# Decoding of the first MoE weight: lower parts on GpSimd, 14 pieces per 18 tiles, one tile between load and first step

## The chip, the cores and the metric

The kernel runs on one core of one Trainium2 chip. The metric is the device time of one execution in microseconds; the figure for the kernel before is the median of three runs. Engines are named as in the profile: PE (TensorE, with PEld for its weight loads), DVE (VectorE), ACT (ScalarE), POOL (GpSimd), SP (SyncE, which here only issues DMAs).

## The reference

An attention with a thresholded softmax, and behind it a two-layer MoE block with a Mish gate:

```python
scores = scale * q @ k.T                      # 8 batches, 8 heads, 576 x 576, head 64
thresh = max(scores) - tau
scores = where(scores >= thresh, scores, -1e9)
attn   = softmax(scores)                      # exp, row sum, division
x      = (attn @ v)  as (4608, 512)
h      = x @ w_in                             # w_in: 512 x 2048
out    = (h * tanh(softplus(h))) @ w_out      # w_out: 2048 x 512
```

q, k and v are given in float32. The two weights are given in float64 and reach the chip as 64-bit words; the chip turns them into float32 itself ("decoding", below).

## The kernel before

**Attention in tiles.** The 64 heads are taken as 32 pairs; a pair gives 9 tiles of 128 x 576 scores, so there are 288 tiles, numbered g. One loop over g (`for g in range(NT + 5)`) issues for each g a bit of work of several tiles in a fixed program order that every compute engine keeps (the wrapper at line 93 chains the instructions of each engine). Per tile: score matmuls on PE into `s`; the row maximum on DVE (`st<-s`); three small DVE operations; the exponential on ACT (`e<-s,st`); the masking with the row sum on DVE (`p<-s,st,e`); the normalisation on POOL (`p<-p,st`, in the next tile); transposes on PE two tiles later (`tp<-ident,p`) and their copies out on ACT (`pf<-tp`; from the fifth pair on `hi<-tp`, with a subtraction `lo<-tp,hi` on DVE); then the product with v on PE. The maximum of tile g+1 stands behind the masking of tile g on DVE.

**The first GEMM.** When the four pairs of a batch are through, `x @ w_in` for it runs as a stream of matmuls that the loop draws from: for tile g of the first batch `MIX_FIRST[(g - 36) % 36]` matmuls, from g = 42 on (6, 14, 22, 6, 16, 4, 12, 4, 15, 9, 16, 13, 7, 12, 5, 10 for tiles 42 to 57). Each product is made from a rounded upper part and a lower part of both factors: three matmuls, `xh*w1h`, `xl*w1h`, `xh*w1l`. So all of `w1h` and `w1l` must be there by the time the stream asks for them. Later the second GEMM, line 848, fills PE to the end.

**The decoding of w_in.** It goes by 32 pieces of 128 x 256 values. A piece needs a buffer `dec` (the pool has five, used in turn: piece i + 5 takes the buffer of piece i), and these steps, each in a tile of its own:

- its load, one DMA on SP's queue, `dec<-w_in` (line 127);
- *first*: two ACT operations (`dec<-dec`);
- *clamp*: one DVE operation; in the next tile *shift* and *sign*, two DVE operations, and *add*, one POOL operation (all `dec<-dec`);
- after one free tile, *upper*: an ACT copy `w1h<-dec`, and *lower*: the subtraction `w1l<-dec,w1h`, on POOL in the same tile or, for the nine pieces named in `ONV`, on DVE one tile later.

A table says in which tiles of each 18 a piece is begun; `LAG` puts empty tiles between the load and *first*:

```python
if weights and g % 18 in W1_STEPS:
    decoding.append([()] * LAG + weights.pop(0)())
...
if d + j * ND in ONV:
    middle = [skip] * 3
    middle[ONP] = lambda: work.lower(nc.vector)
    last = [(work.upper,), middle]
else:
    last = [(lambda: (work.upper(), work.lower(nc.gpsimd)),)]
return [(work.first, skip), *spread(work, STAGES[(d + j) % 2]), *THIRD, *last]
```

With LAG = 2, a piece begun (loaded) in tile s has *first* in s+3, *clamp* in s+4, *shift* and *sign* in s+5, *upper* and *lower* in s+7 (lower in s+8 on DVE). The 32 pieces are begun in tiles 1, 3, 4, 6, 7, 8, 10, 12, 13, 15, 16, 17, and so on by 18, the last in tile 48. The DMA waits for the *lower* of the piece that had the buffer before it.

**Order inside a tile.** ACT: exponential; *first*; copies of y (`x<-y`) and the splits of the next pairs' q, k and v (`q<-r`, `k<-r`); *upper*; the copies out of the transposes. POOL: normalisation; the subtractions of these splits (`q<-r,q`, `k<-r,k`, `vs<-r,vs`, `xl<-x,xh`); *lower*; *add*. DVE: the small operations of the maximum; the reciprocal; *clamp*; *shift*, and before tile 39 (`JOIN`) *sign*; the masking; the maximum of the next tile.

Of the kernel before, what the change touches and what calls it, by code (L numbers as in the profile page):

```python
# [15 lines left out]
B, H, S, D = 8, 8, 576, 64  # L16
NP = H // 2
LOADS = ((1, 0, 1, 3, 2, 3, 7, 3, 5, 8), (0, 3, 3, 2, 5, 4, 5, 8, 5, 7), (0, 0, 2, 4, 5, 4, 7, 6, 7, 8))
W1_STEPS = (1, 3, 4, 6, 7, 8, 10, 12, 13, 15, 16, 17)
STAGES = ((0, 1, 1), (0, 1, 1))  # L20
THIRD = ((),)
LAG = 2
XSPLIT = (4, 1, 2)
ORDER = (0, 0)
PIECES = (3, 3, 3, 3, 4, 2, 3, 4, 3)
# [1 line left out]
FULL = NP  # L27
UNV = 54
ONP = 1
ONV = (3, 9, 11, 12, 14, 15, 17, 18, 22)  # L30
JOIN = 39
PLAIN = (1,)
DM, DF = 512, 2048
# [125 lines left out]
def attention_moe(tc, q, k, v, tau, w_in, w_out, out):  # L159
# [3 lines left out]
    with ExitStack() as outer:  # L163
# [12 lines left out]
        with ExitStack() as first:  # L176
# [6 lines left out]
            with ExitStack() as att:  # L183
# [17 lines left out]
                def decode_w1(d, j):  # L201
# [5 lines left out]
                    work.load(w_in[d * P:(d + 1) * P, sl])  # L207
                    if d + j * ND in ONV:
                        middle = [skip] * 3
# [343 lines left out]
                for g in range(NT + 5):  # L553
# [70 lines left out]
                    for work in loads.pop(g, []):  # L624
                        chores.setdefault(max(g + 2, 2), []).append(work())
                    if weights and g % 18 in W1_STEPS:
                        decoding.append([()] * LAG + weights.pop(0)())
                    if g < NT:
# [270 lines left out]
```

## Time and profile before

| | |
|---|---|
| median of 3 runs | 1373.96 us (1373.25 to 1374.07) |
| profiled execution | 1371.94 us, of which the span of the program's instructions is 1370.2 us |
| granted TensorE clock | 0.996 |
| PE, PEld busy | 99%, 89% |
| DVE, ACT, POOL busy | 73%, 69%, 56% |
| decoding of w_in | from 6.8 us (first load) to about 192 us (last lower part) |

Times inside the execution count from the start of the span. A busy share of the whole span is a mean over stages with different limits, so the stages are read apart in the prediction. A row such as `e<-s,st x288` is a group: the names are the program's (what is written, what is read), then the count. A row of the timeline has start, duration, engine, operation, and in brackets the idle time of the engine before it and what ended that.

### The profile page before, as it was taken

What the parts mean: (1) busy time and instruction counts of PE and PEld (TensorE: products, weight loads), DVE (VectorE), ACT (ScalarE), POOL (GpSimd) and SP (SyncE); (2) the same over time, 40 slices, a digit from 0 to 9 for tenths busy, and PEclk for the clock granted to TensorE, in tenths of its full rate; (3) what the DMA queues carried; (4) which work ended last, traced back from release to release, by engine and by line L of the source; (5) the groups of instructions that cost most, each with busy time, mean ns of one, the idle gap of its engine ahead of it and who ended that gap; (6) DMA issues with size and microseconds to landing.
All of it is one profiled execution on the core that took longest, in us unless ns stands there. A gap on an engine that the chain in (4) does not pass through costs nothing. (4 is left out here: it accounts for less than half of the span.)

```text
span 1370.2 us, 27693 instructions
## 1 busy us (share of the span) xinstructions
PE 1352.5 (99%) x8839; PEld 1225.8 (89%) x8839; DVE 1000.6 (73%) x2976; ACT 944.0 (69%) x2106; POOL 774.0 (56%) x1115
## 2 busy tenths in 40 slices
PE   9998999999999999999999999999999999999999
PEld 7555899999999999999999999999987888888888
DVE  5999999999999999999999999957874332232210
ACT  5788788888888888888888888856555543443210
POOL 4778888778788787887887878732460000000000
PEclk9999999999999999999999999999999999999999
DMA  4333423333333233332332423128655553543310
GB/s 142 100 96 109 121 79 116 108 96 103 101 99 115 89 121 93 111 105 99 103 111 88 121 93 107 64 86 279 194 164 154 150 151 103 143 132 99 95 52 23
DMA packets 126017, 154.64 MB, mean 113 GB/s; under 512 B 23472, under 2 KB 109488, under 8 KB 125872
## 3 DMA queue, kind: packets, MB, share of 16 engines
q1 hardware_dynamic: 124720, 148.16, 36.2%
q10 hardware_dynamic: 1152, 4.72, 0.9%
q8 instruction: 70, 1.15, 0.3%
q14 instruction: 75, 0.61, 0.1%
HBM read 105.64 MB, written 47.19 MB: 112 GB/s over the span
## 5 line engine op out<-in xcount | busy, mean ns | idle before, releaser
L848 PE MATMUL o<-g,w2h 128*128 128x512 f32 (+1 forms) x1280 | 363.7, 370 | 0.6 <-DVE g L681 0.6
L93 PE MATMUL h<-xh,w1h 128*128 128x288 f32 x1024 | 302.3, 295 | 1.0 <-ACT hst L93 0.6
L93 PE MATMUL h<-xl,w1h 128*128 128x288 f32 x1024 | 302.2, 295 | 0.0
L93 PE MATMUL h<-xh,w1l 128*128 128x288 f32 x1024 | 302.2, 295 | 0.0
L93 POOL TENSOR_SCALAR p<-p,st 128x576 f32<-128x576 f32 x288 | 244.9, 850 | 58.6 <-DVE st L93 37.2
L848 PEld LDWEIGHTS o<-g,w2h 128*128 128x128 f32 x1280 | 231.6, 188 | 43.4 <-DVE g L681 1.1
L93 PE MATMUL s<-k,q 128*128 128x288 f32 (+1 forms) x1280 | 255.0, 324 | 7.9 <-DVE p L93 5.8
L93 DVE SCALAR_TENSOR_TENSOR p<-s,st,e 128x576 f32<-128x576 f32 x288 | 235.0, 816 | 20.6 <-ACT e L93 11.0
L93 ACT ACTIVATE e<-s,st 128x576 f32<-128x576 f32 x288 | 214.4, 744 | 35.5 <-DVE st L93 30.2
L848 PE MATMUL o<-g,w2l 128*128 128x512 f32 (+1 forms) x640 | 236.1, 369 | 0.0
L93 DVE TENSOR_REDUCE st<-s 128x1 f32<-128x576 f32 x288 | 216.6, 752 | 6.7 <-PE s L93 6.6
L93 PEld LDWEIGHTS s<-k,q 128*128 128x128 f32 (+1 forms) x1280 | 182.5, 189 | 37.4 <-DVE p L93 21.8
L93 DVE TENSOR_TENSOR lo<-tp,hi 128x512 fp32r<-128x512 f32 (+1 forms) x280 | 174.7, 632 | 48.0 <-ACT hi L93 41.0
L93 PEld LDWEIGHTS h<-xh,w1h 128*128 128x128 f32 x1024 | 192.6, 188 | 1.9 <-ACT hst L93 1.0
L93 PEld LDWEIGHTS h<-xh,w1l 128*128 128x128 f32 x1024 | 192.5, 188 | 0.0
L93 PEld LDWEIGHTS h<-xl,w1h 128*128 128x128 f32 x1024 | 192.5, 188 | 0.0
L93 PE MATMUL tp<-ident,p 128*128 128x128 f32 x1152 | 174.4, 274 | 3.5 <-DVE lo L93 2.3
L93 ACT CAST hi<-tp 128x512 fp32r<-128x512 f32 (+1 forms) x280 | 149.8, 546 | 36.4 <-PE tp L93 33.5
L681 DVE TENSOR_TENSOR g<-ht,g 128x1024 fp32r<-128x1024 f32 (+1 forms) x60 | 68.6, 1153 | 137.6 <-ACT g L680 137.6
L93 PEld LDWEIGHTS tp<-ident,p 128*128 128x128 f32 x1152 | 139.0, 140 | 13.6 <-issue 5.8
L676 ACT ACTIVATE ht<-ht 128x1024 f32<-128x1024 f32 (+1 forms) x60 | 60.2, 1003 | 115.9 <-DMA ht<-hd 114.5
L848 PEld LDWEIGHTS o<-g,w2l 128*128 128x128 f32 x640 | 120.3, 188 | 21.2
(87 smaller groups left out, 2226.7 us busy)
## 6 DMA issues: line engine op xcount, KB each, us to landing
hd<-hst SPq DMA_DIRECT2D x56, 576.0 KB, 3.3
r<-q SPq DMA_DIRECT2D x120, 160.0 KB, 2.3
r<-k SPq DMA_DIRECT2D x120, 160.0 KB, 2.3
ht<-hd SPq DMA_DIRECT2D x52, 288.0 KB, 3.3
r<-v SPq DMA_DIRECT2D x56, 160.0 KB, 2.3
dec<-w_in SPq DMA_DIRECT2D x32, 256.0 KB, 2.7
out_t<-ost SPq DMA_DIRECT2D x32, 256.0 KB, 2.9
g<-w_out SPq DMA_DIRECT2D x48, 128.0 KB, 2.8
```

The source lines that it names most:

```text
L93: made = method(*args, **kwargs)
L676: nc.scalar.activation(ht, ht, AF.Mish)
L681: engine.tensor_tensor(gl, ht, fv(gh), ALU.subtract)
L848: nc.tensor.matmul(o[:, :m], a, b, start=n == 0, stop=n == 3 * NF - 1)
```

## The change

Three constants. The table of tiles in which a piece is begun has 14 entries per 18 tiles instead of 12 (5 and 14 are new), `LAG` is 1 instead of 2, and `ONV` is empty, so that every *lower* is a POOL operation in the tile of *upper*.

```diff
-W1_STEPS = (1, 3, 4, 6, 7, 8, 10, 12, 13, 15, 16, 17)
+W1_STEPS = (1, 3, 4, 5, 6, 7, 8, 10, 12, 13, 14, 15, 16, 17)
...
-LAG = 2
+LAG = 1
...
-ONV = (3, 9, 11, 12, 14, 15, 17, 18, 22)
+ONV = ()
```

A piece begun in tile s now has *first* in s+2, *clamp* in s+3, *shift*, *sign* and *add* in s+4, *upper* and *lower* in s+6. The last piece is begun in tile 41 instead of 48. The number of `dec` buffers stays five.

Two places in the order of the engines. POOL around tiles 8 to 11, before: p is a normalisation (one per tile), q0 the subtraction of a split, `dec_325` the second piece (begun in tile 3), `dec_359` the third.

```order
L93 TENSOR_SCALAR p_519<-p_519,st_500 128x576
L93 TENSOR_TENSOR q0_469<-r_475,q0_469 64x320
L93 TENSOR_TENSOR dec_359<-dec_359 128x256
L93 TENSOR_SCALAR p_519<-p_519,st_539 128x576
L93 TENSOR_TENSOR w1l_97<-dec_325,w1h_96 128x256
L93 TENSOR_SCALAR p_601<-p_601,st_580 128x576
L93 TENSOR_TENSOR w1l_97<-dec_359,w1h_96 128x256
L93 TENSOR_TENSOR dec_431<-dec_431 128x256
```

The same place now, from the normalisation in tile 9; `dec_327` is the second piece.

```order
L93 TENSOR_SCALAR p_529<-p_529,st_510 128x576
L93 TENSOR_TENSOR q0_477<-r_483,q0_477 64x320
L93 TENSOR_TENSOR w1l_97<-dec_327,w1h_96 128x256
L93 TENSOR_TENSOR dec_402<-dec_402 128x256
L93 TENSOR_SCALAR p_529<-p_529,st_549 128x576
L93 TENSOR_TENSOR w1l_97<-dec_360,w1h_96 128x256
L93 TENSOR_TENSOR dec_438<-dec_438 128x256
L93 TENSOR_SCALAR p_617<-p_617,st_593 128x576
L93 TENSOR_TENSOR w1l_97<-dec_402,w1h_96 128x256
L93 TENSOR_TENSOR dec_485<-dec_485 128x256
```

The lower part of the second piece has moved from tile 10 to tile 9, behind the subtraction of q0, and a lower and an add stand in every tile from 9 on where one of them stood before.

ACT from the exponential of tile 9 to that of tile 11, before; `dec_477` and `dec_515` are the fifth and sixth piece (begun in tiles 7 and 8).

```order
L93 ACTIVATE e_540<-s_482,st_539 128x576
L93 ACTIVATE dec_431<-dec_431 128x256 x2
L93 CAST q0_469<-r_475 128x320
L93 COPY pf_566<-tp_530 128x4x128
L93 COPY pf_567<-t5_535 64x128
L93 ACTIVATE e_581<-s_523,st_580 128x576
L93 ACTIVATE dec_477<-dec_477 128x256 x2
L93 COPY x_369<-y_487 64x320
L93 CAST w1h_96<-dec_325 128x256
L93 COPY pf_566<-tp_570 128x4x128
L93 COPY pf_567<-t5_575 64x128
L93 ACTIVATE e_620<-s_560,st_619 128x576
```

The same now; `dec_485` and `dec_525` are the sixth and the seventh piece (begun in tiles 7 and 8).

```order
L93 ACTIVATE e_550<-s_492,st_549 128x576
L93 ACTIVATE dec_485<-dec_485 128x256 x2
L93 CAST q0_477<-r_483 128x320
L93 CAST w1h_96<-dec_327 128x256
L93 COPY pf_579<-tp_540 128x4x128
L93 COPY pf_580<-t5_545 64x128
L93 ACTIVATE e_594<-s_533,st_593 128x576
L93 ACTIVATE dec_525<-dec_525 128x256 x2
L93 COPY x_370<-y_497 64x320
L93 CAST w1h_96<-dec_360 128x256
L93 COPY pf_579<-tp_583 128x4x128
L93 COPY pf_580<-t5_588 64x128
```

In tile 10 ACT now begins the seventh piece, which uses the buffer of the second piece, whose lower part stands on POOL in tile 9; before, it began the fifth there, which had a buffer of its own from the start.

## The prediction

> **What bounds the kernel now.** The time was read in three steps: the page, the windows by stage, then the timeline of the stage that the change touches.
>
> ```profile
> span 1370.2 us, 27693 instructions
> PE 1352.5 (99%) x8839; PEld 1225.8 (89%) x8839; DVE 1000.6 (73%) x2976; ACT 944.0 (69%) x2106; POOL 774.0 (56%) x1115
> ```
>
> PE is busy 99% of the span, so over the whole kernel only PE counts. The decoding lies in the first 192 us, and there the shares differ. Columns are the window, its length, and the busy time of each engine with its count, then granted clock and DMA.
>
> ```profile
> core 0: us, PE busy (x) PEld busy (x) DVE busy (x) ACT busy (x) POOL busy (x), PEclk, DMA share, GB/s
> 20.00:64.00 44.00, 43.82 (x217) 25.78 (x216) 38.48 (x146) 33.87 (x87) 30.41 (x37) 1.00 0.31 87
> 64.00:119.00 55.00, 53.88 (x247) 29.83 (x248) 52.24 (x184) 45.76 (x120) 45.13 (x53) 1.00 0.36 101
> 119.00:135.00 16.00, 14.01 (x72) 8.16 (x69) 14.80 (x54) 13.50 (x34) 12.94 (x15) 1.00 0.37 102
> 135.00:160.00 25.00, 21.73 (x139) 20.23 (x139) 24.44 (x80) 19.83 (x52) 20.41 (x26) 0.86 0.37 113
> 160.00:194.00 34.00, 30.98 (x228) 29.18 (x227) 32.97 (x109) 28.77 (x74) 31.80 (x41) 1.00 0.34 104
> 197.00:253.00 56.00, 55.99 (x432) 55.31 (x431) 51.37 (x168) 47.91 (x117) 45.37 (x69) 1.00 0.33 102
> ```
>
> Up to 194 us DVE is busy 87 to 98% of each window, while PEld is nearly half idle up to 135 us (PE's "busy" there is few long matmuls). From 197 us on PEld is busy 55.31 of 56 us: there PE is the bound, and stays it. So the change is worth what it does to the time at which the loop leaves tile 57; what follows is the same PE work. The loop's clock is the exponential of each tile, on ACT; here those of tiles 18, 36, 41, 47, 57, 58 and 76.
>
> ```profile
> 63.41 0.74 ACT L93 ACTIVATE e<-s,st 128x576 f32<-128x576 f32 x1 [1.60 <-DVE st L93]
> 119.09 0.74 ACT L93 ACTIVATE e<-s,st 128x576 f32<-128x576 f32 x1 [1.50 <-DVE st L93]
> 135.38 0.74 ACT L93 ACTIVATE e<-s,st 128x576 f32<-128x576 f32 x1
> 159.55 0.77 ACT L93 ACTIVATE e<-s,st 128x576 f32<-128x576 f32 x1
> 194.38 0.74 ACT L93 ACTIVATE e<-s,st 128x576 f32<-128x576 f32 x1
> 197.62 0.74 ACT L93 ACTIVATE e<-s,st 128x576 f32<-128x576 f32 x1
> 253.04 0.74 ACT L93 ACTIVATE e<-s,st 128x576 f32<-128x576 f32 x1
> ```
>
> Tiles 18 to 35 take 55.68 us (3.09 each), tiles 41 to 56 take 59.00 (3.69 each), tiles 58 to 75, PE-bound, 55.42 (3.08 each). The prices of the decoding's steps (min/median/max in ns) come from the view of its buffer:
>
> ```profile
> L93 DVE TENSOR_SCALAR dec<-dec x64: 273/325/1051, 23.5 to 182.5; 128x256 f32<-128x256 f32 x32, 128x256 uint32<-128x256 uint32 x32
> L93 DVE SCALAR_TENSOR_TENSOR dec<-dec x32: 410/840/2282, 26.4 to 184.0; 128x256 uint32<-128x256 uint32 x32
> L93 POOL TENSOR_TENSOR dec<-dec x32: 726/738/977, 27.3 to 185.0; 128x256 uint32<-128x256 uint32 x32
> L93 POOL TENSOR_TENSOR w1l<-dec,w1h x23: 722/737/974, 33.6 to 191.1; 128x256 fp32r<-128x256 f32 x23
> L93 DVE TENSOR_TENSOR w1l<-dec,w1h x9: 409/413/954, 50.7 to 140.8; 128x256 fp32r<-128x256 f32 x9
> DMA to landing us min/median/max: 2.5/2.7/5.0
> ```
>
> **Part 1: more pieces before tile 41.** Counting clamps by the table, 24 pieces are clamped before tile 41 now and 29 after the change; by tile 36 it is 21 and 25. What a piece costs a tile is read between tiles 18 and 36. The next rows, around tiles 17 to 20, serve this part and part 3.
>
> ```profile
> 61.42 0.89 POOL L93 TENSOR_TENSOR w1l<-dec,w1h 128x256 fp32r<-128x256 f32 x1
> 62.34 0.33 SPq L127 DMA_DIRECT2D dec<-w_in  x1
> 64.05 0.76 ACT L93 ACTIVATE dec<-dec 128x256 f32<-128x256 f32 x2
> 65.29 0.88 POOL L93 TENSOR_TENSOR q<-r,q 64x320 fp32r<-64x320 f32 x1 [0.59 <-DVE p L93]
> 65.97 0.74 ACT L93 ACTIVATE e<-s,st 128x576 f32<-128x576 f32 x1 [0.17 <-DVE st L93]
> 66.61 0.78 ACT L93 ACTIVATE dec<-dec 128x256 f32<-128x256 f32 x2
> 68.52 0.75 ACT L93 ACTIVATE e<-s,st 128x576 f32<-128x576 f32 x1
> 69.16 0.78 ACT L93 ACTIVATE dec<-dec 128x256 f32<-128x256 f32 x2
> ```
>
> Exponentials of tiles 18, 19 and 20 are at 63.41, 65.97, 68.52: a tile in which the decoding fits beside the exponential takes 2.56. Eighteen of those are 46.1; the measured 55.68 is 9.6 more, for 12 pieces: 0.8 us a piece. Between 4 and 5 more pieces before tile 41: **+3.6** (bounds +2 and +5; the upper one if each pays all its DVE work, 0.27 + 0.27 + 0.41 = 0.95 undisturbed).
>
> **Part 2: lower parts off DVE.** Nine times 0.41 leaves DVE: at most -3.7. Nine times 0.74 = 6.6 us goes to POOL. What that gives back is a matter of waits between the two engines, seen around tiles 6 and 11:
>
> ```profile
> 26.37 0.43 DVE L93 SCALAR_TENSOR_TENSOR dec<-dec 128x256 uint32<-128x256 uint32 x1
> 40.17 0.73 POOL L93 TENSOR_TENSOR w1l<-dec,w1h 128x256 fp32r<-128x256 f32 x1 [0.29 <-ACT w1h L93]
> 40.65 0.60 DVE L93 TENSOR_SCALAR dec<-dec 128x256 f32<-128x256 f32 x2
> 40.91 0.96 POOL L93 TENSOR_SCALAR p<-p,st 128x576 f32<-128x576 f32 x1
> 41.28 0.85 DVE L93 SCALAR_TENSOR_TENSOR dec<-dec 128x256 uint32<-128x256 uint32 x1
> ```
>
> The same sign takes 0.43 us or 0.85 us; the long one begins at 41.28, inside a normalisation on POOL (40.91 to 41.87). Clamp and shift, begun 0.25 us before a lower on POOL ends, take only 0.60 together for 2 x 0.27. The Trainium skill, page "SBUF — State Buffer", section "Who interferes with whom", states that DVE and GpSimd share one pair of ports as an exclusive lock, and that the one that issues second waits for the whole instruction of the other; the doubled sign agrees. By that rule the edit trades a DVE operation of 0.41 that holds off POOL for a POOL operation of 0.74 that holds off DVE. Without it: the gain lies between -3.7 and, if each moved lower delays one DVE operation by half its 0.74 instead, 0.37 x 9 = +3.3. I take **-1.5**, nearer to the gain, since the rows at 40.65 show a lower on POOL costing DVE about 0.1.
>
> **Part 3: loads that come too late.** A load waits for the lower of the piece five before. Row 61.42 shows a lower of tile 17 ending at 62.31, and row 62.34 the load it releases; this piece's first is at 69.16, in tile 20, and with 2.7 to land it has some 4 us to spare. With the new table the distance between that lower and first is two tiles or more for 23 of the 27 pieces that wait; for those begun in tiles 8, 17, 26 and 35 it is one: the lowers stand in tiles 9, 18, 27, 36, and first in the tile behind. In each of these four tiles a subtraction of q stands ahead of the lower on POOL. In tile 18 it ends at 65.29 + 0.88 = 66.17; a lower behind it ends at 66.9, its load lands at 69.6. First in tile 19 was due at 66.61, or about 67.2 once tile 18 carries clamp, shift and sign and lasts 3.15 rather than 2.56. So ACT, which works in order, stands for 2.4 us with the copies out of the transposes and the next exponential queued behind it. From first to the next exponential it needs 68.52 - 66.61 = 1.91, so that comes at 71.5; undisturbed it would come 3.15 after an exponential at 66.6, at 69.7. Of the 1.8 the tile hides 0.6, the DVE work by which it would overrun anyway (3.15 - 2.56). Four times 1.2: **+4.8** (from +2, ACT and POOL running ahead, to +8, nothing hidden). On SP no other load that is due soon stands behind the four: the next ones there serve pieces two tiles on and splits four tiles on or later.
>
> **Part 4: tiles 41 to 57.** Eight pieces are clamped here now, three after the change, none of them behind tile 44. What is left is PE's own work. With the weight load as the price of a matmul of the first GEMM,
>
> ```profile
> L93 PEld LDWEIGHTS h<-xh,w1h 128*128 128x128 f32 x1024 | 192.6, 188 | 1.9 <-ACT hst L93 1.0
> ```
>
> a round of 18 tiles (192 matmuls) needs 36.1 us of the 55.42 measured; the other 19.3, 1.07 a tile, is attention. Tiles 42 to 47 hold 68 matmuls: 12.8 + 6.4 = 19.2 us, or 22.3 at the clock of 0.86 granted in that window, against 24.17 measured (135.38 to 159.55): -2. Tiles 48 to 57 hold 103: 19.4 + 10.7 = 30.1 against 34.83 (159.55 to 194.38); a lower part left in tile 47 and the odd wait keep 1 of it: -3.5. Together **-5.5** (bounds -9, all of 59.0 down to 16 x 1.07 + 171 x 0.188 = 49.3 and a little back, and -3).
>
> **Part 5: POOL in tiles 18 to 40.** Of the nine lowers seven stood on DVE in tiles 18 to 36. They and four operations of two more pieces add 11 x 0.74 = 8.1 to the 45.13 of the second window: 53 of 55 us. The worst tile is 32, where four splits fall together:
>
> ```profile
> 107.86 1.68 POOL L93 TENSOR_TENSOR k<-r,k 128x320 fp32r<-128x320 f32 x2 [0.46 <-ACT k L93]
> 109.50 0.91 POOL L93 TENSOR_TENSOR vs<-r,vs 128x320 fp32r<-128x320 f32 x1
> 110.37 0.99 POOL L93 TENSOR_TENSOR xl<-x,xh 128x288 fp32r<-128x288 f32 x1
> ```
>
> To these 3.5 us now come a lower and an add, 1.5. Normalisations slip, but transposes need them two tiles later: **+1.5** (0 to +5).
>
> **Sum.** 3.6 - 1.5 + 4.8 - 5.5 + 1.5 = +2.9 us. The profiled execution took 1371.94 (span 1370.2, 1.7 around it), 2.0 below the median of the runs; the difference is added to the median: 1373.96 + 2.9, rounded **1377 us**.
>
> **Rivals.** *The stalls are covered, and the early tiles take the extra pieces cheaply* (faster). ACT is idle 9 of 55 us in the second window and might absorb most of each stall: parts 1 to 5 become 3.0 - 3.0 + 1.6 - 6.5 + 0 = -4.9, 1369 us. For it: part 4's gain is plain in PE's idle time. Against: ACT's order is fixed, and a stall of 2.4 in a tile of 3.15 exceeds its idle share. Chance 0.20.
>
> *POOL becomes the bound* (clearly slower). At 53 of 55 us each clamp and sign finds POOL in the middle of something, as the sign of 0.85 does, and pays the +3.3 of part 2 instead of -1.5; tiles 30 to 39 then follow POOL, part 5 at +5. It decides where a tile's POOL work exceeds about 3.1 us. Sum +11, or with the bounds not all at once +8: 1382. This is also what the exclusive lock of the Trainium skill, page "SBUF — State Buffer", section "Who interferes with whom", would make of the change. Against: the rows at 40.65. Chance 0.20.
>
> *Nothing measurable*: part 3 at half, +2.4, leaves +0.5: 1374.5. Chance 0.15. That the change does not do what it says is excluded by the order of the engines, but for the four loads that it does not bring a tile ahead.
>
> **The numbers.** The forecast keeps 0.45. Something under 0.2%, 2.7 us, cannot be told from no change here. The forecast's own spread is about 3 us around +2.9, a little over half of it above 2.7: 0.27 slower, 0.18 same. So slower 0.47, same 0.33, faster 0.20. The range runs from the middle of the faster rival, 1369, to just above the POOL rival, 1383; it leaves out half of the first and a third of the second.
>
> **What would show it.** Right: four idle times of ACT of about 2 us before *first* in tiles 10, 19, 28 and 37, ended by the DMA `dec<-w_in`; exponential 41 about 8 us later than 135.4, and 57 about 3 later than 194.4; no PE idle behind tile 48. Wrong: ACT's waits on that DMA under 0.5 us each (part 3 falls, and the time goes below 1374); exponentials 18 to 36 further apart than 62 us (POOL's rival); tiles 48 to 57 still above 33 us (part 4 falls, time above 1380).

## The result and the profile after

| | before | after |
|---|---|---|
| median of the runs, us | 1373.99 (1373.25 to 1374.07, 4 runs) | 1394.67 (1389.09 to 1400.17, 4 runs) |
| after / before | | 1.0153, 95% interval 1.0133 to 1.0173 |
| profiled execution, us | 1371.94 at a mean clock of 0.996 | 1399.05 at a mean clock of 0.985 |

The change makes the kernel slower by 1.3 to 1.7%. The direction is the one forecast, the size is not: 1394.67 stands above the range's end of 1383. The four runs of after are 1399.05, 1389.09, 1390.29 and 1400.17 us, at mean granted clocks of 0.985, 0.992, 0.991 and 0.985: one program whose time goes with the clock. The profiled execution is one of the two long ones, so its trace shows more of the loss than the median has.

The page of after, its span, its engines and the slices of the granted clock:

```profile
span 1397.2 us, 27714 instructions
PE 1367.7 (98%) x8839; PEld 1231.1 (88%) x8839; DVE 1002.3 (72%) x2967; ACT 944.1 (68%) x2106; POOL 773.8 (55%) x1124
PEclk9698999999999999999999999999999999999999
```

PE has 15.2 us more of busy time for the same 8839 matmuls (1352.5 before), and the second and fourth slice, about 35 to 70 and 105 to 140 us, stand at 6 and 8. The windows by stage show what that means (columns as in the prediction):

```profile
core 0: us, PE busy (x) PEld busy (x) DVE busy (x) ACT busy (x) POOL busy (x), PEclk, DMA share, GB/s
20.00:44.00 24.00, 21.67 (x109) 12.84 (x107) 21.78 (x80) 16.77 (x45) 13.53 (x17) 1.00 0.21 58
44.00:68.00 24.00, 23.78 (x57) 11.77 (x58) 11.16 (x40) 12.12 (x31) 13.64 (x18) 0.50 0.30 80
68.00:119.00 51.00, 42.82 (x200) 23.76 (x198) 44.23 (x146) 34.99 (x93) 33.20 (x43) 1.00 0.29 81
119.00:130.00 11.00, 11.00 (x27) 5.09 (x26) 6.41 (x21) 6.40 (x17) 9.69 (x13) 0.53 0.40 116
165.00:194.00 29.00, 24.72 (x165) 23.83 (x164) 26.59 (x88) 21.72 (x57) 23.94 (x30) 0.88 0.29 87
194.00:222.00 28.00, 27.72 (x210) 26.73 (x209) 25.91 (x91) 23.95 (x57) 21.69 (x29) 1.00 0.30 97
224.00:280.00 56.00, 56.00 (x433) 55.30 (x432) 51.38 (x169) 47.91 (x117) 45.24 (x69) 1.00 0.32 102
```

From 44 to 68 us the granted clock is 0.50. PE is busy 23.78 of 24 us and gets through 57 matmuls, where the 24 us before hold 109; DVE, 91% busy before, falls to 11.16 of 24 us. In these tiles PE is the bound. From 119 to 130 the same again. From 224 on everything is as it was before: 433 matmuls in 56 us.

The four idle times that the prediction named are there. On ACT, *first* of tiles 10, 19, 28 and 37, with the idle time before it in brackets:

```profile
42.23 0.76 ACT L93 ACTIVATE dec<-dec 128x256 f32<-128x256 f32 x2 [2.76 <-DMA dec<-w_in]
...
83.97 0.76 ACT L93 ACTIVATE dec<-dec 128x256 f32<-128x256 f32 x2 [2.72 <-DMA dec<-w_in]
...
116.40 0.76 ACT L93 ACTIVATE dec<-dec 128x256 f32<-128x256 f32 x2 [3.46 <-DMA dec<-w_in]
...
153.38 0.76 ACT L93 ACTIVATE dec<-dec 128x256 f32<-128x256 f32 x2 [2.36 <-DMA dec<-w_in]
```

What follows the first of them is read from the timeline of all engines, tile 10 to tile 13:

```profile
38.41 0.73 POOL L93 TENSOR_TENSOR w1l<-dec,w1h 128x256 fp32r<-128x256 f32 x1
...
39.17 7.77 SPq L127 DMA_DIRECT2D dec<-w_in  x3
...
41.80 0.79 PE L93 MATMUL s<-k,q 128*128 128x288 f32 x4 [0.86 <-DVE p L93]
...
44.13 0.74 ACT L93 ACTIVATE e<-s,st 128x576 f32<-128x576 f32 x1
44.22 1.09 PE L93 MATMUL tp<-ident,p 128*128 128x128 f32 x4 [1.62 <-ACT pf L93]
...
47.96 4.13 PE L93 MATMUL s<-k,q 128*128 128x288 f32 x8
...
52.03 1.11 PE L93 MATMUL tp<-ident,p 128*128 128x128 f32 x4
```

The lower part of the second piece ends at 39.14, the load it releases is issued at 39.17 (a row that merges three issues) and *first* begins at 42.23. Behind it wait the copies out of the transposes, and PE cannot put the next transposes anywhere: it stands for 1.62 us, until ACT's copy `pf`. The 0.86 us of idle time ahead of that are not the late load's: they end with DVE's masking, `p`, and that stands behind a clamp and a shift that take 1.30 us together and a sign of 0.93, while POOL does a lower and an add (38.41 to 39.89):

```profile
38.74 1.30 DVE L93 TENSOR_SCALAR dec<-dec 128x256 f32<-128x256 f32 x2
40.08 0.93 DVE L93 SCALAR_TENSOR_TENSOR dec<-dec 128x256 uint32<-128x256 uint32 x1
40.93 0.81 DVE L93 SCALAR_TENSOR_TENSOR p<-s,st,e 128x576 f32<-128x576 f32 x1
```

At 44.22 the transposes come back, and they now take 1.09 us. Four such transposes in before, on PE:

```profile
52.24 0.66 PE L93 MATMUL tp<-ident,p 128*128 128x128 f32 x4
```

So a late load stops ACT, ACT stops PE, and PE, which had stood once already for DVE, then runs on at half clock: from 44.0 for 23.9 us, and after the third late load from 119.1 for 10.2 us. After the second and the fourth the clock stays. Two more halvings of 3.4 us follow, at 166.9 and 177.1. In before the granted clock is halved for 3.4 us at 8.9 and for 6.8 us at 135.2.

The exponentials of tiles 18, 36, 41, 47 and 57 in after:

```profile
77.37 0.74 ACT L93 ACTIVATE e<-s,st 128x576 f32<-128x576 f32 x1 [1.47 <-DVE st L93]
...
146.81 0.74 ACT L93 ACTIVATE e<-s,st 128x576 f32<-128x576 f32 x1 [1.68 <-DVE st L93]
...
165.19 0.74 ACT L93 ACTIVATE e<-s,st 128x576 f32<-128x576 f32 x1
...
190.33 0.74 ACT L93 ACTIVATE e<-s,st 128x576 f32<-128x576 f32 x1 [0.16 <-DVE st L93]
...
221.43 0.74 ACT L93 ACTIVATE e<-s,st 128x576 f32<-128x576 f32 x1
```

Against before they are 14.0, 27.7, 29.8, 30.8 and 27.1 us late: what is lost in this execution is lost by tile 41, and what tiles 41 to 57 give back is 2.8 us.

### The profile page after: what moved, and what is told of

Read it like the earlier page. It is cut to its first block, busy times and chain, and to the rows that moved or that the text cites. A ratio compares the mean times of both kernels' runs of the same rounds, so it can differ in the third digit from the quotient of the medians.

```text
span 1397.2 us, 27714 instructions
## 1 busy us (share of the span) xinstructions
PE 1367.7 (98%) x8839; PEld 1231.1 (88%) x8839; DVE 1002.3 (72%) x2967; ACT 944.1 (68%) x2106; POOL 773.8 (55%) x1124
## 4 chain that ended last, share of the span: by engine, by line
PE 84%; DVE 4%; ACT 4%; DMA 3%; issue 2%; POOL 2%; SPq 1%; ACTq 0%; DVEq 0%; POOLq 0%
PE h L93 26%; PE o L848 23%; PE s L93 13%; PE y L93 11%; PE tp L93 9%; PE t L93 1%; DMA dec<-w_in 1%; DVE g L93 1%; DVE st L93 1%; DVE p L93 1%; POOL w2l L156 1%; DVE dec L93 1%; DMA g<-w_out 1%; ACT dec L93 1%; ACT e L93 0%
## 5 line engine op out<-in xcount | busy, mean ns | idle before, releaser
L93 POOL TENSOR_SCALAR p<-p,st 128x576 f32<-128x576 f32 x288 | 240.5, 835 | 62.9 <-DVE st L93 42.7
L93 PE MATMUL s<-k,q 128*128 128x288 f32 (+1 forms) x1280 | 261.1, 329 | 14.4 <-DVE p L93 13.1
L848 PEld LDWEIGHTS o<-g,w2h 128*128 128x128 f32 x1280 | 231.7, 188 | 43.6 <-DVE g L681 1.7
L93 PEld LDWEIGHTS s<-k,q 128*128 128x128 f32 (+1 forms) x1280 | 185.5, 192 | 48.3 <-DVE p L93 30.2
L93 POOL TENSOR_TENSOR x<-x,yo 64x256 f32<-64x256 f32 (+1 forms) x112 | 89.6, 800 | 88.6 <-ACT yo L93 85.6
```

Source lines behind the costliest of these rows:

```text
L93: made = method(*args, **kwargs)
L848: nc.tensor.matmul(o[:, :m], a, b, start=n == 0, stop=n == 3 * NF - 1)
```

## The experiments

The theory after the result: the four late loads cost little by ACT's delay and much by the halved clock that PE's idle time brings. Its rivals: the late loads cost that much by themselves (ACT's order); the lower parts on POOL cost it, because DVE's operations take longer beside them; the denser table costs it. Start times in us of the exponentials, by tile, from the profiled execution of each kernel, for all that follows:

| kernel | 11 | 14 | 18 | 36 | 41 | 57 |
|---|---|---|---|---|---|---|
| before | 40.6 | 51.3 | 63.4 | 119.1 | 135.4 | 194.4 |
| after | 44.1 | 61.9 | 77.4 | 146.8 | 165.2 | 221.4 |
| even table | 41.0 | 51.2 | 64.5 | 124.7 | 143.0 | 198.9 |
| lower parts only | 40.8 | 51.5 | 63.6 | 119.4 | 136.3 | 195.9 |
| PE filled at the late loads | 44.8 | 54.6 | 68.0 | 132.7 | 152.0 | 206.7 |
| table only | 41.4 | 51.6 | 63.7 | 123.8 | 144.8 | 200.0 |
| all but the table | 40.2 | 50.4 | 62.4 | 120.0 | 136.7 | 199.0 |
| the same, one late load | 44.3 | 60.0 | 71.9 | 129.5 | 146.2 | 203.8 |
| LAG only | 41.0 | 51.2 | 63.2 | 121.2 | 137.9 | 199.7 |
| score matmuls of 41 and 42 doubled | 40.8 | 51.5 | 63.6 | 119.2 | 135.5 | 193.8 |
| lower one tile earlier | 42.0 | 51.9 | 64.6 | 127.0 | 145.1 | 199.4 |

Each row is one execution. The runs of before range from 1370.69 to 1378.32 us, so a difference of 1 or 2 us between two rows says little by itself.

**After with 14 pieces per 18 tiles, but spaced so that no lower stands one tile before the *first* that needs its buffer.**

```diff
-W1_STEPS = (1, 3, 4, 5, 6, 7, 8, 10, 12, 13, 14, 15, 16, 17)
+W1_STEPS = (1, 2, 3, 4, 6, 7, 8, 10, 11, 12, 13, 15, 16, 17)
```

> The changed kernel with its 14 pieces spread evenly, so that no piece's first step stands one tile behind the lower part that frees its buffer (always two or more). Theory (late loads idle PE, the granted clock is halved, PE becomes the bound): ACT does not wait for dec<-w_in, the clock stays at 1.0 between tiles 10 and 36, exponential 41 comes at 135 to 145 us, time 1369 to 1377 us. Rival (the lower parts and the extra pieces crowd GpSimd and VectorE): the time stays above 1385 us, with exponential 41 beyond 155 us.

Measured: 1377.83 us (1377.12 to 1378.60), ratio to before 1.0038 (1.0023 to 1.0053). ACT does not wait for a load in tiles 10, 19, 28 or 37; mean clocks 0.994 to 0.996, with halvings of 3.4 us at 104.2 and 6.8 us at 141.8. The first of these was not expected, and the time is 0.83 us above the range; exponential 41, at 143.0, is within it. Three quarters of the loss hang on where in the table the two new pieces stand, not on their number and not on where the lower parts run.

**Before with the lower parts on POOL, nothing else.**

```diff
-ONV = (3, 9, 11, 12, 14, 15, 17, 18, 22)
+ONV = ()
```

> The kernel before with all lower parts on GpSimd and nothing else. Theory: no late load arises (distance between lower and first step as before or longer), so no more than a few us either way: 1370 to 1377 us. Rival (crowding of GpSimd): 1380 us or more, with VectorE's sign operation at 0.84 us or longer throughout.

Measured: 1373.23 us (10 runs, 1371.56 to 1374.36), ratio 0.9998 (0.9988 to 1.0007): no difference. The view of the buffer `dec` in this kernel (min/median/max in ns) shows where the time on DVE went:

```profile
L93 DVE TENSOR_SCALAR dec<-dec x64: 272/391/2420, 23.7 to 182.5; 128x256 f32<-128x256 f32 x32, 128x256 uint32<-128x256 uint32 x32
L93 DVE SCALAR_TENSOR_TENSOR dec<-dec x32: 414/846/972, 26.5 to 185.6; 128x256 uint32<-128x256 uint32 x32
L93 POOL TENSOR_TENSOR w1l<-dec,w1h x32: 718/736/890, 33.8 to 192.7; 128x256 fp32r<-128x256 f32 x32
```

The median of clamp and shift rises from 325 to 391 ns, the longest from 1.05 to 2.42 us. Added up over all clamps, shifts, signs and lowers, DVE spends 55.3 us on the decoding here and 55.6 in before: nearly all of the 3.7 us that nine lowers of 0.41 take away comes back as longer durations of the others.

**After with the PE idle time filled.** The score matmuls of tiles 12, 21, 30 and 39, which PE issues while ACT waits for the late load, are issued three times; the result is the same, PE's work grows by four times 8 matmuls, about 1 us each time. The kernel of before fills PE in the same way up to tile 9, with 85 transposes `warm<-ident` of which nothing is used (1.4 to 38.2 us); tile 10, with the first late load, is the first tile without them.

```diff
-                def scores(t, first, qs, k1, k2, plain, **_):
+                def scores(t, first, qs, k1, k2, plain, times=1, **_):
...
-                    for c in range(2):
+                    for c in [0, 1] * times:
...
-                    tiles[g] = dict(s=scores(t, D if g % 2 == 0 else 0, **made))
+                    tiles[g] = dict(s=scores(t, D if g % 2 == 0 else 0, times=3 if g in (12, 21, 30, 39) else 1, **made))
```

> The changed kernel with the score matmuls of tiles 12, 21, 30 and 39 issued three times (the result is the same), so that PE has some 1.6 us more of work in each of the four stalls. Theory: ACT still waits 2.3 to 3.5 us for the same four loads, but the clock is not halved for longer than 7 us at a time, and the time falls to 1376 to 1382 us. If the stalls alone cost the time, or crowding does, it stays at 1389 us or more.

Measured: 1386.44 us (1385.56 to 1387.22), ratio 1.0100 (1.0085 to 1.0115); the mean clock is 0.996 in every run. ACT's waits are as in after; here the row of the view of waits (sum, times, longest) of this kernel,

```profile
ACT dec L93 <- DMA dec<-w_in: 11.6, 4, 3.2
```

and that of after:

```profile
ACT dec L93 <- DMA dec<-w_in: 11.7, 5, 3.5
```

On PE the idle time around the first of them has shrunk from 0.86 + 1.62 to 0.86 + 0.57 us,

```profile
42.48 1.84 PE L93 MATMUL s<-k,q 128*128 128x288 f32 x12 [0.86 <-DVE p L93]
44.89 0.63 PE L93 MATMUL tp<-ident,p 128*128 128x128 f32 x4 [0.57 <-ACT pf L93]
```

and the transposes behind it take 0.63 us, not 1.09. The window from 44 to 68 us of this kernel:

```profile
44.00:68.00 24.00, 22.21 (x103) 12.27 (x102) 20.56 (x70) 18.66 (x50) 18.92 (x24) 1.00 0.41 115
```

The granted clock is 1.0 and DVE does 70 instructions where after does 40. With the same late loads and more work on PE the kernel is 8 us faster than after, and its runs no longer scatter. The clock is halved once behind 20 us, for 6.8 us at 151.3, near the place where before has it too. Only the work in PE's idle time differs from after, so the idle time is what brings the long half clocks. But 1386.44 is above the 1376 to 1382 expected; the late loads cost more than ACT's forecast delay with the clock kept, too.

**Before with the table alone.** LAG stays 2 and the nine lowers stay on DVE.

```diff
-W1_STEPS = (1, 3, 4, 6, 7, 8, 10, 12, 13, 15, 16, 17)
+W1_STEPS = (1, 3, 4, 5, 6, 7, 8, 10, 12, 13, 14, 15, 16, 17)
```

> The kernel before with the table of 14 pieces only; LAG and the lower parts on VectorE as before. Theory: the late loads come from the table and the five buffers, not from LAG (both the lower part that frees a buffer and the first step move by it), so they are here too, two of them later still where the lower part is VectorE's, one tile later: at least four waits of ACT for dec<-w_in over 1.5 us, a halved clock behind them, 1388 us or more. Rival (the shorter lead of LAG = 1, or the crowding by the lower parts, is the cause): under 1380 us.

Measured: 1383.13 us (10 runs, 1377.29 to 1390.31), ratio 1.0075 (1.0052 to 1.0098); at least 1388 was expected. The runs lie in two groups: 1377.29 to 1380.08 us at clocks of 0.996 to 0.993 (five runs) and 1386.18 to 1390.31 at 0.988 to 0.985 (five runs). The profiled execution is the fastest, and loads are late in it too, three of them by more than 1.5 us (1.81, 2.80 and 2.97, in tiles 11, 29 and 38), where at least four were expected:

```profile
ACT dec L93 <- DMA dec<-w_in: 8.6, 5, 3.0
```

Its clock is not halved before 140 us. So the late loads come with the table and the five buffers, not with LAG: freeing lower and waiting *first* both move with it. The five executions at the higher clocks lie 3.2 to 6.0 us above before's 1374.12, with the additional pieces in it, so late loads cost little there. Between the groups the time goes with the clock; where it was halved in the longer executions no trace shows.

**Before with the score matmuls of tiles 41 and 42 doubled** (the same code with `times=2 if g in (41, 42)`), to see what the halved clock of before, 6.8 us from 135.2, costs there.

```diff
+                    tiles[g] = dict(s=scores(t, D if g % 2 == 0 else 0, times=2 if g in (41, 42) else 1, **made))
```

> The kernel before with the score matmuls of tiles 41 and 42 issued twice (same result; 1.6 us more PE work), where PE stands idle 0.9, 1.1 and 1.3 us between 131 and 136 us and the clock is halved from 135 to 142 us. Theory (idle PE halves the clock, and that costs more than the idle time): the clock is not halved there, and the time is 1 to 3 us shorter, 1371 to 1373 us. Rival (the clock does not matter there, other engines set the pace): the same time or 1 to 2 us more.

Measured: 1372.60 us (10 runs, 1371.13 to 1374.90), ratio 0.9998 (0.9988 to 1.0007). The clock is no longer halved at 135 us (1.0 from 12.3 on), exponential 57 comes at 193.8 instead of 194.4, and the time does not move. The gain of 1 to 3 us is not there: this short halving costs nothing that shows. What the doubled matmuls themselves cost was not told apart from it. In after the half clock costs where PE becomes the bound by it.

**Before with all of the change but the table.**

```diff
-LAG = 2
+LAG = 1
...
-ONV = (3, 9, 11, 12, 14, 15, 17, 18, 22)
+ONV = ()
```

> The kernel before with LAG = 1 and all lower parts on GpSimd: the change without its table. Theory (the table with five buffers makes the late loads; LAG moves the freeing lower part and the first step alike): no wait of ACT for dec<-w_in over 0.5 us, 1370 to 1377 us. Rival (the load is too late because it is one tile closer to its first step): four or more such waits and 1385 us or more.

Measured: 1377.35 us (6 runs, 1375.92 to 1378.79), ratio 1.0034 (1.0022 to 1.0047), at the upper end of what the theory gave. No load is late. Up to tile 41 it loses 1.3 us, behind it 3.3 more: tile 52 alone takes 6.1 us, for a reason that the run of LAG alone shows below.

**The same, with one more piece, begun in tile 5,** which makes exactly one late load, in tile 10.

```diff
-                    if weights and g % 18 in W1_STEPS:
+                    if weights and (g % 18 in W1_STEPS or g == 5):
```

> The kernel of e8 with one piece more, begun in tile 5: exactly one late load, in tile 10, the last piece two tiles earlier. By the price of the prediction, 1.2 us for the stall, it takes what e8 takes plus 1 to 2 us in every execution. By the clock theory the executions differ among each other: 2 us more where the clock stays, 4 to 8 us more and a clock at or below 0.992 where it is halved behind tile 10, so the spread is over 4 us.

Measured: 1382.35 us (1379.97, 1382.09, 1382.61 and 1388.14 at clocks of 0.995, 0.993, 0.993 and 0.989), ratio 1.0077 (1.0052 to 1.0102). In the profiled execution ACT waits 2.77 us in tile 10 and the clock is halved from 43.6 for 13.7 us. The window from 43 to 57 us of this kernel,

```profile
43.00:57.00 14.00, 12.64 (x30) 6.23 (x31) 7.19 (x24) 7.66 (x20) 9.08 (x12) 0.52 0.25 70
```

and of the one without the late load:

```profile
43.00:57.00 14.00, 14.00 (x62) 7.65 (x62) 12.32 (x47) 11.33 (x31) 10.94 (x14) 1.00 0.39 110
```

Half the matmuls, half of DVE's work. The two kernels differ by 5.0 us in the median (1382.35 - 1377.35), 2.6 in the fastest and 10.8 in the slowest run, where the prediction had 1.2; a spread of over 4 us is what the clock theory expected. But the late load costs more than this difference. Exponential 11 is 4.1 us later than without it, 14 is 9.5 later, and every one from there to 52 is 9.5 to 9.6 later: nothing of it is taken up again. Only exponential 57 is 4.8 later, because tiles 52 to 54 are short here, where the kernel without the late load has its tile of 6.1 us; with one piece more, begun earlier, the last piece comes two tiles sooner. Of the 9.5 us, 1.7 are there before the stall (exponential 10).

**Before with LAG = 1 alone.**

```diff
-LAG = 2
+LAG = 1
```

> The kernel before with LAG = 1 alone, lower parts on VectorE as before. If the 4 us that LAG = 1 and the empty list took together come from LAG (the decoding meets the fifth pair's splits in other tiles): 1376 to 1379 us. If they come from the two together, or from where VectorE happens to stand behind several GpSimd operations: 1371 to 1375 us. No wait of ACT for dec<-w_in over 0.5 us in either.

Measured: 1375.71 us (10 runs, 1372.98 to 1378.12), ratio 1.0019 (1.0010 to 1.0029), with no late load: it costs about 2.6 us, between the two expectations. The profiled execution is the slowest of the ten (1378.12), so it shows more than the median has. The place is tile 52 again, 6.1 us long; DVE and POOL in its timeline:

```profile
180.69 0.81 POOL L93 TENSOR_SCALAR p<-p,st 128x576 f32<-128x576 f32 x1
...
181.03 2.88 DVE L93 TENSOR_SCALAR dec<-dec 128x256 uint32<-128x256 uint32 x1
...
181.48 0.79 POOL L93 TENSOR_TENSOR xl<-x,xh 128x288 fp32r<-128x288 f32 x1
...
182.24 0.85 POOL L93 TENSOR_TENSOR k<-r,k 128x320 fp32r<-128x320 f32 x1
...
183.05 0.71 POOL L93 TENSOR_TENSOR w1l<-dec,w1h 128x256 fp32r<-128x256 f32 x1
```

A shift that takes 0.27 us undisturbed begins inside a normalisation on POOL and ends at 183.91, when POOL has finished this and three more instructions (183.76). With LAG = 1 the shift of this piece stands one tile earlier than in before, and there it meets that row of four. That the shift waited for POOL is read from these times alone.

**After with the lower part one tile earlier.** The free tile between *add* and *upper* with *lower* is taken out; every buffer is then free at least two tiles before its *first*.

```diff
-THIRD = ((),)
+THIRD = ()
```

> The changed kernel, its table kept, without the empty tile between add and upper/lower, so that each buffer is free one tile earlier and every load is released at least two tiles ahead of its first step. Theory (late loads, and the clock behind them, make most of the 20 us): no wait of ACT for dec<-w_in over 1 us, no halved clock between tiles 10 and 36, 1374 to 1380 us, like the evenly spread table. Rival (14 pieces in 18 tiles in bunches crowd VectorE and GpSimd whatever the loads do): 1385 us or more.

Measured: 1377.68 us (7 runs, 1376.32 to 1378.23), ratio 1.0031 (1.0019 to 1.0042), clocks 0.995 to 0.998. ACT has no wait on a load of `dec`; the table of 14 and all else is as in after. The clock is halved once between tiles 10 and 36, for 3.4 us at 106.1, where no halving was expected. By the ratios (1.0153 and 1.0031) the late loads and what they bring are worth 17 us of the 21; the rest of the change still costs 4.3. A sixth `dec` buffer, the other way to take the late loads away, was not tried.

No version is faster than before.

## Why the prediction was wrong

**The step that failed is the price in part 3**, "four times 1.2: +4.8 (from +2, ACT and POOL running ahead, to +8, nothing hidden)". The waits themselves were forecast rightly: four of 2.4 us forecast, 2.76, 2.72, 3.46 and 2.36 measured, at the four places named, and the direction, slower, came for this reason. But the price was taken from ACT's delay of the next exponential alone, with PE as an engine that has room there. PE stood as well, the granted clock went to 0.5, and PE became the bound of tiles 11 to 15 and 29 to 31: tile 13 takes 8.05 us (53.82 to 61.87) after 4.08 in before. The prediction had quoted a granted clock of 0.86 in before, between 135 and 160 us, and used it only as a price of part 4; what brings it, and that the stalls could bring it again, as two of the four did, it didn't ask. The sum has no term for it. By ratios: without late loads (lower one tile earlier) 1.0031; with them and the clock kept (PE filled) 1.0100, that is +9.4 us at most, since the 32 added matmuls, some 4 us of PE, are in it; with the clock halved 1.0153, another +7.3 at least, since after is without these matmuls. Together that is some 17 us where part 3 had 4.8 and at most 8. Between single executions the clock's part runs from 2.6 us (1389.09) to 13.7 (1400.17) above the filled kernel.

**Part 1 and part 5** (3.6 and 1.5) were too low. Five more pieces make exponential 41 come 9.8 us later with the lower one tile earlier and 7.6 with the even table, of which LAG and ONV without the table make 1.3. That is 1.3 to 1.7 us a piece, not 0.8: the price was read from tiles 18 to 36 of before as a mean, and the additional pieces come into tiles that are probably full already, which no run tests by itself. How it divides between parts 1 and 5 was not tested either.

**Part 2**, -1.5, is 0: 0.9998 (0.9988 to 1.0007). The rows at 40.65, one pair of clamp and shift that lost only 0.06 to POOL, were no measure for the others. The prediction's other sign, the one of 0.43 us that it set against the long one "inside a normalisation on POOL", begins inside a normalisation as well:

```profile
26.25 1.08 POOL L93 TENSOR_SCALAR p<-p,st 128x576 f32<-128x576 f32 x1 [0.72 <-DVE st L93]
```

There the POOL instruction is the long one, so where the sign begins did not tell which engine would wait.

**Part 4**, -5.5, is near right where no load is late: with the lower one tile earlier, tiles 41 to 56 take 54.2 us instead of 59.0, -4.8. In after it is -2.8: from exponential 47 to 57 3.7 us are gained, as forecast (3.5, for "tiles 48 to 57"), but tiles 41 to 46 lose 1.0 instead of gaining 2. Two short halvings of the clock lie there, and this pair of clamp and shift on DVE, among POOL's work in tile 43:

```profile
173.00 0.74 POOL L93 TENSOR_TENSOR x<-x,yo 64x256 f32<-64x256 f32 x1
...
173.19 3.23 DVE L93 TENSOR_SCALAR dec<-dec 128x256 f32<-128x256 f32 x2
...
173.70 0.80 POOL L93 TENSOR_TENSOR xl<-x,xh 128x288 fp32r<-128x288 f32 x1
...
174.50 0.94 POOL L93 TENSOR_SCALAR p<-p,st 128x576 f32<-128x576 f32 x1
175.41 0.85 POOL L93 TENSOR_TENSOR vs<-r,vs 128x320 fp32r<-128x320 f32 x1
```

It should take 0.55 us. PE stands 2.39 us behind it (174.81 to 177.20), and the second of the two halvings follows.

**The rivals.** The stalls were not covered. POOL did not become the bound: POOL is busy 33.20 of 51 us from 68 to 119, less than in before's second window, and the sign's median is 846 ns against 840. But after has stalls there, so the better test is the kernel without late loads, lower one tile earlier, between exponentials 18 and 36; here before and this kernel:

```profile
63.41:119.09 55.68, 54.56 (x254) 30.31 (x253) 52.88 (x188) 46.34 (x120) 45.51 (x53) 1.00 0.36 101
64.64:126.99 62.35, 56.50 (x253) 31.08 (x251) 57.79 (x188) 48.29 (x127) 50.55 (x63) 0.97 0.35 99
```

POOL is busy 82% and 81%, DVE 95% and 93%: POOL is no more the bound than before. The test that the prediction set for that rival, exponentials 18 to 36 further apart than 62 us, came true (69.4) mostly for another reason; it is met by a hair, 62.35, without late loads too. A distance between two tiles does not tell which engine made it. What the additional pieces cost in these tiles, and the 0.86 us for which PE stood for DVE ahead of the first late load's own 1.62, are what is left of the crowding that this rival had in mind. The prediction's test of part 4, tiles 48 to 57 within 33 us, was met (31.1 us, 190.33 to 221.43), and no PE idle time is left behind tile 48 (27.72 of 28 us busy).

## What to carry to other kernels

When a wait is priced, follow it past the engine that waits to PE, even in a stage that PE does not bound: if PE stands there for a microsecond or two, look whether the granted clock falls behind it and whether PE would be the bound at half of it. In a ring of buffers, count for every piece the time from the step that frees its buffer to the step that needs it, with the load's 2.7 us between; a table that is denser in the mean can be too early at a few places, and spacing the same 14 pieces otherwise took back three quarters of the loss here. Taking nine short operations off DVE gained nothing here, as the others took longer with the replacements on POOL. And when two variants are compared to price one thing, compare them tile by tile: the 5.0 us of the single late load hid half of its cost, because the other kernel lost time elsewhere.

## What the runs showed of the hardware that was not expected

**The half clock lasts.** At idle times of PE of 0.86 and 1.62 us that lie within 3.3 us (40.94 to 44.22), the clock fell, and it stayed at half for 23.9 us although PE was busy 23.78 of 24.00 us; in other kernels for 13.7 and 10.2, in others for 3.4. Nor does every such idle time bring it. The half clocks last 3.4, 6.8, 10.2, 13.7 or 23.9 us in these traces, all multiples of 3.41 us, and within a trace the changes lie on one raster with this step. It matters how PE's idle time falls on it. In after, the step ahead of the first halving, and the two steps on which the idle time of the second late load falls (0.86 and 1.59 us, from 82.71 to 85.97):

```profile
40.60:44.00 3.40, 1.13 (x6) 0.56 (x4) 3.01 (x12) 1.77 (x6) 0.47 (x2) 1.00 0.18 63
81.50:84.90 3.40, 2.01 (x9) 0.95 (x7) 3.37 (x12) 0.93 (x3) 1.02 (x2) 1.00 0.36 112
84.90:88.30 3.40, 2.33 (x11) 1.17 (x11) 2.13 (x9) 2.80 (x8) 2.88 (x5) 1.00 0.28 74
```

PE is busy 1.13 of 3.40 us in the first, and the clock falls; it is busy 2.01 and 2.33 us in the others, and the clock stays. Ahead of 119.1 it is busy 1.07 us, ahead of 135.2 in before 1.42. So whether a stall halves the clock is in part luck of the raster, which may be why the runs of the kernel with the table alone split five to five; that is not shown. In the eleven traces, from 20 to 200 us, each of the 16 steps at full clock in which PE is busy for half of the step or less is followed by a halving. Of the steps in which it is busy for more, only three are: their halvings last 3.4 us and follow steps in which PE was busy about nine tenths (104.2 in the even table, 73.7 with LAG alone, 106.1 with the lower one tile earlier), for a reason that stays open. The Trainium skill, page "TensorE: Matmul & The Clock Gate", section "Part 1: The HAM clock gate (the "warmup" mystery)", states that an idle window of about 3.4 us halves the clock, that about 3.4 us of sustained activity restores it, and that the window runs freely, so that it varies between runs. The variation agrees; the 23.9 us of a busy PE at half clock do not, and PE was busy for a third of the 3.40 us ahead of the first halving. What PE would have to do to get its clock back sooner stays open.

**DVE waits across several POOL instructions.** A shift of 0.27 us took 2.42 us with the lower parts on POOL and 2.88 with LAG alone, the second across the rest of one POOL instruction and three whole ones. Before has it too: its longest sign, 2.28 us from 141.99, ends behind three POOL instructions. The Trainium skill, page "SBUF — State Buffer", section "Who interferes with whom", states that, of two instructions that need the ports which DVE and GpSimd share, the one that comes second waits for the whole instruction of the other; the wait agrees, but here it did not end with that one instruction.
